# A recurrence and a feed-forward block in one kernel: keys kept in a ring in SBUF, block inverses taken round by round, weights with four landing buffers

## The chip, the cores and the metric

The kernel runs on one core of a Trainium2 chip. A core has TensorE (matrix products; its weight loads are a queue of their own in the profile), VectorE, ScalarE, GpSimd and SyncE (which issues the transfers here), each of which takes its instructions in order. The metric is the device time of one execution in microseconds (us), lower is better.

## The reference

Two blocks follow each other. The first is a recurrence over 768 positions with a 40x40 state for each of 4 x 8 heads; the second takes its output as 3072 rows of 320.

```python
for t in range(S):                                    # S = 768, heads of D = 40
    y[:, :, t] = einsum('bhd,bhde->bhe', rt, state)
    Sa = einsum('bhde,bhe->bhd', state, at)
    state = state * wt[:, :, None, :] - einsum('bhd,bhe->bhde', Sa, bt) \
            + einsum('bhd,bhe->bhde', vt, kt)
x = y.transpose(0, 2, 1, 3).reshape(B * S, H * D)     # (3072, 320)
h = x @ w_in                                          # d_ff = 1024
e = exp(h - max(h))
solu = h * (e / (sum(e) + 1e-9))
ln = (solu - mean(solu)) / sqrt(var(solu) + 1e-6) * g_ln
out = ln @ w_out
```

The arrays r, k, v, w, a, b come in 32-bit floats. w_in and w_out come as 64-bit floats, which the kernel reads as pairs of 32-bit words and converts itself.

## The kernel before

The 768 positions are cut into 12 rounds of 64 (chunks). The loop has 24 iterations: iteration i takes round i // 2 for two of the four batches. Within a chunk the recurrence becomes matrix products and the inverse of a unit triangular matrix of 64x64 for each head; its two 32x32 diagonal blocks are inverted on VectorE (`invert`), and the rest is put together by products (`solve`).

The parts of one iteration are Python generators; each `next` emits one piece, and a string of letters gives the order in which the pieces go into the engines' queues: r recurrence, f (and g) front, a attend (for i + 1), s solve (for i + 1), h hidden, I invert, W weights. `front` runs AHEAD = 7 iterations ahead and makes the keys `kx` (two scaled keys, A^T, decays); hidden and output run LAG = 4 iterations behind.

```python
AHEAD, LAG = 7, 4
kx_t = [const.tile([P, KW + G * AXW], FP32, name=f"kx{i}") for i in range(2)]

def spill(i):                     # keys go to DRAM ...
    d["kx_dram"] = dram.tile([P, KW + G * AXW], FP32, tag="kx_dram", name="kx_dram")
    nc.sync.dma_start(out=d["kx_dram"], in_=d["kx"])

def bring(i):                     # ... and come back when they are needed
    kx = two.tile([P, KW + G * AXW], FP32, tag="kxx", name="kxx")
    nc.sync.dma_start(out=kx, in_=d["kx_dram"])

def invert(number, got):          # rounds 0 and 1 alone on 64 partitions, then two rounds on 128
    # ... u = -nb, diagonal 1
    for j in range(1, Q - 1):     # Q = 32
        m = Q - 1 - j
        nc.vector.tensor_tensor(out=t, in0=nb[:, j:j + 1, j + 1:Q].to_broadcast([n_, j, m]),
                                in1=u[:, 0:j, j:j + 1].to_broadcast([n_, j, m]), op=ALU.mult)
        nc.vector.tensor_tensor(out=u[:, 0:j, j + 1:Q], in0=u[:, 0:j, j + 1:Q], in1=t, op=ALU.subtract)
        yield
    # ... transposed copy, both to DRAM, to be brought back in another layout

def weights():                    # 12 pieces of w_in, 16 of w_out
    def fetch(j):
        bits[j] = two.tile([P, 512], I64, tag=("e", "lnT")[j % 2], name="bits", bufs=1)
        # ... transfer of piece j into it
    fetch(0)
    fetch(1)
    yield
    for j, (dst, _, by) in enumerate(pieces):
        new = narrow(dst, bits[j], by)     # conversion: VectorE, ScalarE, then GpSimd
        # ... first half of new, second half of the piece before
        if j:
            fetch(j + 1)
        yield

def hidden(i):                    # two pieces h = x w_in (second with the maximum), then
    # yield; exponential (ScalarE); yield
    nc.vector.tensor_tensor(out=q, in0=h, in1=e, op=ALU.mult)
    for half in range(2):
        nc.vector.bn_stats(out=bs[:, half], in_=q[:, half * 512:half * 512 + 512])
    nc.vector.bn_aggr(out=mv, in_=bs)
    # ... four operations on one column; yield; ln; yield

STEADY = "r I f h r a f a h a r r h f r f h a s h a r s a"
EARLY = "r f r I W a f a g a I W r r g f r f I W a s g a r I W s g a"
# each iteration: turns(EARLY if i < LAG else STEADY, dict(I=count, W=3), **parts),
# then spill, readout(i), bring(i + 2), repack, scatter, rest of invert, output(i - LAG), store
```

In the profile the tensors carry these names: pcum, pcx, paT, pbT, pnt are products of front (its steps); px with sm and pu, psT, pnu, pst, plamu those of recurrence; pyo that of its crossed part and of readout; pkT, pvT, prT, ppsi, plamv, px with psi of attend; py, pz of solve; h, plnT, po of the feed-forward; bits are landed weights; blk, prod, u belong to invert.

Of the kernel before, what the change touches and what calls it, by code (L numbers as in the profile page):

```python
# [17 lines left out]
P = 128  # L18
Q = 32
L = 64  # L20
TILE_HEADS = ((0, 4, 3), (1, 5, 7), (2, 6))
AHEAD = 7
LAG = 4
# [30 lines left out]
def kernel(  # L54
# [22 lines left out]

# [12 lines left out]
    raw = ctx.enter_context(tc.tile_pool(name="raw", bufs=2))  # L90
    two = ctx.enter_context(tc.tile_pool(name="two", bufs=2))
    small = ctx.enter_context(tc.tile_pool(name="small", bufs=4))
    dram = ctx.enter_context(tc.tile_pool(name="dram", bufs=AHEAD + 2, space=bass.MemoryType.DRAM))
# [38 lines left out]
    kx_t = [const.tile([P, KW + G * AXW], FP32, name=f"kx{i}") for i in range(2)]  # L132
# [6 lines left out]
    tn_t = [const.tile([P, 2, G, Q], FP32, name=f"tinv{i}") for i in range(2)]  # L139
    sm_t = zeroed(nc.vector, "sm", [P, 2, G, 64], 2)  # L140
    st_t = [const.tile([P, 2, G, D], FP32, name=f"st{i}") for i in range(2)]
    nu_t = [const.tile([P, H, 64], FP32, name=f"nu{i}") for i in range(2)]
# [13 lines left out]
    def narrow(dst, land, by=None):  # L156
# [3 lines left out]
        flat = land.bitcast(I32)  # L160
        word = flat[0:n, 0:2 * width].rearrange("p (n two) -> p n two", two=2)
        low, hi = word[:, :, 0], word[:, :, 1]
        man, scale = flat[0:n, 1024 - width:1024], flat[0:n, 1024 - 2 * width:1024 - width]
# [15 lines left out]
    def weights():  # L179
# [18 lines left out]
        bits = {}  # L198

        def fetch(j):  # L200
            if j >= len(pieces):
                return
            dst, parts = pieces[j][:2]
            n, width = dst.shape
            to = dst
            if not exact:
                bits[j] = two.tile([P, 512], I64, tag=("e", "lnT")[j % 2], name="bits", bufs=1)
                to = bits[j][0:n, 0:width]
            row = 0
            for part in parts:  # L210
                nc.sync.dma_start(out=to[row:row + part.shape[0]], in_=part)
                row += part.shape[0]

        fetch(0)
        fetch(1)
        yield
        open_ = None
        for j, (dst, _, by) in enumerate(pieces):
            new = None
            if not exact:  # L220
                new = narrow(dst, bits[j], by)
            elif by is not None:
                nc.gpsimd.tensor_scalar(out=dst, in0=dst, scalar1=by[0], scalar2=None, op0=ALU.mult)
# [4 lines left out]
            if j:  # L228
                fetch(j + 1)
# [41 lines left out]
    def wide(name, bufs=2):  # L271
# [4 lines left out]
    blocks, inverse = {}, {}  # L276
# [25 lines left out]
    def group(n):  # L302

        return (n, 0, 1) if n < 2 else (1 + n // 2, n % 2, 2)

    def decay(i):

        d = st[i]
        lw, kx = lw_t[i % 2], kx_t[i % 2]
        d["kx"] = kx  # L310
        d["kb"], d["ax"] = kb, ax = split(kx)
        nc.scalar.activation(out=keyed(lw)[:, :, :, 0:D], in_=by_heads(given(i, "w")), func=AF.Ln)
# [21 lines left out]
    def homes(n, q, s=None):  # L334

        _, place, rounds = group(n)
        at = (q * rounds + place) * 2 * H + (s or 0) * H
        return slice(at, at + (H if s is not None else 2 * H))

    def front(i):  # L340
# [25 lines left out]
        if s == 0:  # L366
            of_round[n]["nt"] = two.tile([P, 2, 2, G, L], FP32, tag="nt", name="nt", bufs=4)
# [3 lines left out]
    def spill(i):  # L371

        d = st[i]
        d["kx_dram"] = dram.tile([P, KW + G * AXW], FP32, tag="kx_dram", name="kx_dram")
        nc.sync.dma_start(out=d["kx_dram"], in_=d["kx"])

    def scatter(n):

        number, place, _ = group(n)
        if place == 0:  # L380
            blocks[number] = dram.tile([P, Q, Q], FP32, tag="blk_dram", name="blk_dram", bufs=2)
        nt = of_round[n]["nt"].rearrange("q s p g t -> q (s p g) t")
        for q in range(4):
            nc.sync.dma_start(out=blocks[number][homes(n, q)].rearrange("h s t -> s h t"),
                              in_=nt[quarter(q), :, quarter(q % 2)])

    first = [two.tile([P, Q, Q], FP32, tag=tag, name=tag, bufs=1) for tag in ("blk", "u")]

    def gather(number):

        if number < 2:
            at = half(number)
            tiles = [x[at] for x in first]
        else:
            at = slice(0, P)
            tiles = [two.tile([P, Q, Q], FP32, tag=tag, name=tag, bufs=1) for tag in ("blk", "u")]
        nc.sync.dma_start(out=tiles[0], in_=blocks[number][0:at.stop - at.start])
        return tiles, at

    def invert(number, got):  # L400

        (nb, u), at = got
        n_ = at.stop - at.start
        flat = u.rearrange("p s t -> p (s t)")
        nc.vector.tensor_scalar(out=flat, in0=nb.rearrange("p s t -> p (s t)"), scalar1=-1.0, scalar2=None,
                                op0=ALU.mult)
        nc.vector.memset(flat[:, 0:Q * Q:Q + 1], 1.0)
        yield
        for j in range(1, Q - 1):
            m = Q - 1 - j  # L410
            t = two.tile([P, Q * Q // 4], FP32, tag="prod", name="prod", bufs=1)[at, 0:j * m] \
                .rearrange("p (c r) -> p c r", c=j)
            nc.vector.tensor_tensor(out=t, in0=nb[:, j:j + 1, j + 1:Q].to_broadcast([n_, j, m]),  # L413
                                    in1=u[:, 0:j, j:j + 1].to_broadcast([n_, j, m]), op=ALU.mult)
            nc.vector.tensor_tensor(out=u[:, 0:j, j + 1:Q], in0=u[:, 0:j, j + 1:Q], in1=t, op=ALU.subtract)  # L415
            yield
        nc.vector.tensor_copy(out=nb, in_=u.rearrange("p s t -> p t s"))
        inverse[number] = []
# [396 lines left out]
```

## Time and profile before

| | before |
|---|---|
| median of three runs | 1035.88 us (1030.49 to 1040.53) |
| span of the profiled run | 1030.6 us, mean granted TensorE clock 0.789 |
| TensorE, weight loads | 708.4 us busy (69%), 529.2 us (51%) |
| VectorE, ScalarE, GpSimd | 420.1 us (41%), 273.4 us (27%), 135.2 us (13%) |
| transfers | 106.75 MB, mean 104 GB/s |

The page cuts the span into 40 equal slices of 25.8 us; each digit is the busy share of a slice in tenths, for PEclk the clock that was granted to TensorE, in tenths of full speed.

```profile
PE   4248143541423869888788887888898888877875
DVE  2865112083221347433276332674337533332231
PEclk9657565755555889888988999788988888888988
DMA  9587613826142354463744636342534223020000
```

The rows are read against each other: a slice in which TensorE has a low digit and no other engine a high one is a slice in which all wait for something.

The costliest groups (line, engine, operation, out <- in with shapes, count | busy us, mean ns of one | idle us ahead of it, and what ended most of that):

```profile
L621 PE MATMUL h<-w_in,xT 120*128 120x512 f32 (+1 forms) x288 | 139.8, 624 | 9.8 <-DVE e L631 6.9
L661 PE MATMUL po<-w,lnT 128*128 128x320 f32 x384 | 112.0, 445 | 4.3 <-ACT lnT L657 4.0
L415 DVE TENSOR_TENSOR u<-u,prod 128x30 f32<-128x30 f32 (+29 forms) x210 | 74.3, 354 | 7.2
L413 DVE TENSOR_TENSOR prod<-blk,u 128x30 f32<-128x30 f32 (+29 forms) x210 | 72.5, 345 | 6.8
```

### The profile page before, as it was taken

The numbers are of one execution on the slowest core, as the hardware profiler recorded it, in microseconds if no ns is written. First come the engines' busy times: TensorE is split into PE (matmuls) and PEld (weight loads), VectorE is DVE, ScalarE is ACT, GpSimd is POOL, SyncE is SP. The second block draws the span as 40 slices with busy tenths as digits, with TensorE's granted clock in tenths as the row PEclk, the third lists the DMA queues.
The fourth block names the chain that finished last, engine by engine and source line by source line (L and its number), as shares of the span: only waits on it lengthen the run. The fifth ranks groups of instructions, "written<-read, shape, count | busy, mean of one in ns | idle before, by whom it ended". The sixth has DMA issues, their size and how long they took to land.

```text
span 1030.6 us, 27637 instructions
## 1 busy us (share of the span) xinstructions
PE 708.4 (69%) x12265; PEld 529.2 (51%) x12265; DVE 420.1 (41%) x941; ACT 273.4 (27%) x592; POOL 135.2 (13%) x202
## 2 busy tenths in 40 slices
PE   4248143541423869888788887888898888877875
PEld 3236133431322647676566665666566566655443
DVE  2865112083221347433276332674337533332231
ACT  3013133200432223223322333233332222221111
POOL 2102032101322110111011110111100000000000
PEclk9657565755555889888988999788988888888988
DMA  9587613826142354463744636342534223020000
GB/s 144 152 227 186 121 36 121 171 103 140 39 132 56 100 116 121 124 151 93 162 100 128 159 100 131 116 121 92 142 82 102 86 75 83 12 66 2 26 13 13
DMA packets 233862, 106.75 MB, mean 104 GB/s; under 512 B 216840, under 2 KB 223056, under 8 KB 227600
## 3 DMA queue, kind: packets, MB, share of 16 engines
q1 hardware_dynamic: 233600, 104.76, 40.9%
q8 instruction: 96, 1.57, 0.6%
q10 hardware_dynamic: 144, 0.23, 0.1%
q14 instruction: 22, 0.18, 0.1%
HBM read 62.30 MB, written 38.73 MB: 98 GB/s over the span
## 4 chain that ended last, share of the span: by engine, by line
PE 43%; DVE 14%; issue 13%; DMA 11%; SPq 9%; ACT 5%; POOL 4%; POOLq 0%; DVEq 0%; ACTq 0%
PE h L621 10%; PE po L661 7%; SPq L292 4%; PE px L467 4%; DMA bits<-in_moe_w_out_dram 4%; PE pyo L592 4%; DVE prod L413 2%; DVE u L415 2%; PE plamu L265 2%; PE pz L489 2%; PE plnT L656 2%; DMA bits<-in_moe_w_in_dram 2%; DMA blk<-blk_dram 2%; DVE e L647 2%; PE pst L565 2%
## 5 line engine op out<-in xcount | busy, mean ns | idle before, releaser
L621 PE MATMUL h<-w_in,xT 120*128 120x512 f32 (+1 forms) x288 | 139.8, 624 | 9.8 <-DVE e L631 6.9
L661 PE MATMUL po<-w,lnT 128*128 128x320 f32 x384 | 112.0, 445 | 4.3 <-ACT lnT L657 4.0
L661 PEld LDWEIGHTS po<-w,lnT 128*128 128x128 f32 x384 | 72.8, 194 | 38.5 <-ACT lnT L657 9.4
L621 PEld LDWEIGHTS h<-w_in,xT 120*128 120x128 f32 (+1 forms) x288 | 54.6, 199 | 64.5 <-issue 62.0
L624 DVE TENSOR_REDUCE nmax<-h 128x1 f32<-128x1024 f32 x24 | 29.3, 1222 | 117.7 <-PE h L621 117.5
L415 DVE TENSOR_TENSOR u<-u,prod 128x30 f32<-128x30 f32 (+29 forms) x210 | 74.3, 354 | 7.2
L413 DVE TENSOR_TENSOR prod<-blk,u 128x30 f32<-128x30 f32 (+29 forms) x210 | 72.5, 345 | 6.8
L326 PE MATMUL pcx<-cst,lw 128*128 128x132 f32 x192 | 38.4, 340 | 45.3 <-ACT kT L249 25.2
L514 PE MATMUL pyo<-rT,sT 64*64 64x64 f32 x704 | 30.3, 295 | 52.5 <-DVE psi L267 52.2
L326 PEld LDWEIGHTS pcx<-cst,lw 128*128 128x128 f32 x192 | 31.9, 235 | 50.9 <-ACT kT L249 28.5
L319 POOL TENSOR_TENSOR kx<-raw_b,inv 128x320 f32<-128x320 f32 x24 | 20.8, 865 | 260.1 <-ACT inv L317 248.5
L503 ACT ACTIVATE tinvT<-pz 32x256 f32<-32x256 f32 x48 | 17.9, 374 | 138.3 <-PE pz L489 138.0
L467 PE MATMUL px<-v,psi 64*64 64x40 f32 x768 | 46.4, 305 | 11.8 <-ACT tinvT L503 11.8
L572 POOL TENSOR_TENSOR st<-tot,kxx 128x320 f32<-128x320 f32 x20 | 14.9, 744 | 295.6 <-DVE tot L571 295.6
L599 DVE TENSOR_TENSOR x<-pyo,kxx 128x512 f32<-128x512 f32 x24 | 16.6, 691 | 89.6 <-PE pyo L592 89.6
L165 DVE TENSOR_SCALAR bits<-bits 128x160 int32<-128x160 int32 (+2 forms) x28 | 7.4, 264 | 111.7 <-DMA bits<-in_moe_w_out_dram 60.2
L514 PEld LDWEIGHTS pyo<-rT,sT 64*64 64x64 f32 x704 | 23.7, 192 | 55.8 <-DVE psi L267 55.3
L657 ACT COPY lnT<-plnT 128x512 f32<-128x512 f32 x48 | 26.4, 588 | 91.3 <-PE plnT L656 91.2
L467 PEld LDWEIGHTS px<-v,psi 64*64 64x64 f32 x768 | 42.8, 220 | 14.2 <-ACT tinvT L503 12.9
L265 PE MATMUL plamu<-rT,nuT 64*64 64x64 f32 x768 | 25.0, 298 | 29.8 <-DVE lamv L267 21.5
L532 DVE TENSOR_TENSOR x<-x_own,px 128x320 f32<-128x320 f32 x22 | 10.7, 485 | 73.7 <-PE px L530 73.7
L664 ACT COPY osb<-po 128x320 f32<-128x320 f32 x24 | 10.2, 425 | 108.0 <-PE po L661 57.6
(106 smaller groups left out, 1292.1 us busy)
## 6 DMA issues: line engine op xcount, KB each, us to landing
kx_dram<-kx SPq DMA_DIRECT2D x24, 1032.0 KB
kxx<-kx_dram SPq DMA_DIRECT2D x24, 1032.0 KB
raw_w<-in_w_dram SPq DMA_DIRECT2D x24, 160.0 KB
raw_b<-in_b_dram SPq DMA_DIRECT2D x24, 160.0 KB
raw_a<-in_a_dram SPq DMA_DIRECT2D x24, 160.0 KB
raw_k<-in_k_dram SPq DMA_DIRECT2D x24, 160.0 KB
v<-in_v_dram SPq DMA_DIRECT2D x24, 160.0 KB
r<-in_r_dram SPq DMA_DIRECT2D x24, 160.0 KB
```

What stands on the lines that cost most here:

```text
L265: nc.tensor.matmul(t[half(c), p, g * L:(g + 1) * L], lhsT=lhs[half(p), g, half(c)], rhs=rhs[half(p), g, half(c)], start=True, stop=True)
L292: nc.sync.dma_start(out=to[half(c)], in_=ap[2 * c:2 * c + 2, :, n * L:(n + 1) * L, :] .rearrange("b h t d -> t (b h) d"))
L326: nc.tensor.matmul(t[:, g * 132:g * 132 + 132], lhsT=pair(lw, 2 * j + g), rhs=cst[:, lo:lo + 132], start=True, stop=True)
L413: nc.vector.tensor_tensor(out=t, in0=nb[:, j:j + 1, j + 1:Q].to_broadcast([n_, j, m]), in1=u[:, 0:j, j:j + 1].to_broadcast([n_, j, m]), op ...
L415: nc.vector.tensor_tensor(out=u[:, 0:j, j + 1:Q], in0=u[:, 0:j, j + 1:Q], in1=t, op=ALU.subtract)
L467: nc.tensor.matmul(t[half(c), h * D:h * D + D], lhsT=psi[half(c), h // G, h % G, :], rhs=given(i, "v")[half(c), h, 0:D], start=True, stop= ...
L514: nc.tensor.matmul(d["y"][half(p), c, g * L:g * L + L], lhsT=d["sT"][half(z), c, m, half(p)], rhs=d["rT"][half(z), (G * p + g) // 2, half(c)],
L592: nc.tensor.matmul(t[half(p), c, g * L:g * L + L], lhsT=kb[half(c), j, 2 * g + p, :], rhs=lam[half(c), h % 2, h // 2, :], start=i < 2 and ...
L621: nc.tensor.matmul(h[:, hh], lhsT=of_round[i // 2]["xT"][0:n, kt, i % 2 * P:i % 2 * P + P], rhs=w_in[0:n, kt, hh], start=kt == 0, stop=kt ...
L624: nc.vector.tensor_reduce(out=nmax, in_=h, axis=AX.X, op=ALU.max, negate=True)
L657: nc.scalar.copy(out=lnT[:, fs.start:fs.stop].rearrange("p f t -> p (f t)"), in_=t)
L661: nc.tensor.matmul(o[:, 0:DM], lhsT=lnT[:, f, :], rhs=w2[:, f, :], start=f == 0, stop=f == NF - 1)
```

## The change

The change keeps the keys on the chip and orders the pieces anew.

- The keys kx live in a ring of AHEAD + 1 = 6 tiles (AHEAD is now 5), so that spill and bring go. To make room, several tiles have one buffer less (raw loads, psi, nuT, tot, sm, nu).
- The inverse is taken once per round (12 times). Each 32x32 block lies on two partitions, its even rows in the lower half of the partitions and its odd rows in the upper half, so one operation covers (j + 1) // 2 rows where it covered j.
- The weights have four landing quarters and two sets of temporaries, three loads are in flight ahead, and the pieces are spread over more iterations (LAG is now 6, so the feed-forward starts two iterations later).
- The feed-forward's product, statistics and small operations are pieces of their own; readout has a letter (y) within the order; the state's update comes after readout, and attend's psi and lamv come late.

```diff
-AHEAD = 7
-LAG = 4
+AHEAD = 5
+LAG = 6
-    raw = ctx.enter_context(tc.tile_pool(name="raw", bufs=2))
+    raw = ctx.enter_context(tc.tile_pool(name="raw", bufs=1))
-    kx_t = [const.tile([P, KW + G * AXW], FP32, name=f"kx{i}") for i in range(2)]
+    kx_t = [const.tile([P, KW + G * AXW], FP32, name=f"kx{i}") for i in range(AHEAD + 1)]
 ... weights
-                bits[j] = two.tile([P, 512], I64, tag=("e", "lnT")[j % 2], name="bits", bufs=1)
+            for tag in ("e", "lnT"):
+                x = two.tile([P, 512], I64, tag=tag, name="bits", bufs=1)
+                land += [x[:, 0:256], x[:, 256:512]]
+            temps = [two.tile([P, 2, 256], I32, tag=tag, name="parts", bufs=1) for tag in ("osb", "parts")]
-        fetch(0)
-        fetch(1)
+        for j in range(3):
+            fetch(j)
-                new = narrow(dst, bits[j], by)
+                new = narrow(dst, land[j % 4], temps[j % 2], by)
-            if j:
-                fetch(j + 1)
+            fetch(j + 3)
 ... spill and bring removed; gather brings a round's blocks twice, once for each half of the partitions
+        for p in range(2):
+            nc.sync.dma_start(out=nb[half(p)], in_=of_round[n]["blocks"])
 ... invert
-            m = Q - 1 - j
+            m, rows = Q - 1 - j, (j + 1) // 2
-                                    in1=u[:, 0:j, j:j + 1].to_broadcast([n_, j, m]), op=ALU.mult)
+                                    in1=u[:, 0:rows, j:j + 1].to_broadcast([P, rows, m]), op=ALU.mult)
+        nc.sync.dma_start(out=ut_dram, in_=ut)
+        for p in range(2):
+            nc.sync.dma_start(out=u_dram.rearrange("b (c z) t -> b c z t", z=2)[:, :, p], in_=u[half(p)])
 ... bring_inverse: tinv in four transfers where there were two, of 16 elements where there were 32
 ... recurrence: crossed part and lamu ahead of the state's update (they came after it)
 ... hidden
         nc.vector.tensor_tensor(out=q, in0=h, in1=e, op=ALU.mult)
+        yield
 ... bn_stats
+        yield
 ... order of the pieces
-    STEADY = "r I f h r a f a h a r r h f r f h a s h a r s a"
-    EARLY = "r f r I W a f a g a I W r r g f r f I W a s g a r I W s g a"
+    FIRST = "r f r I a f a g a r r g f r f I s g y s I r a g a I f g a"
+    EARLY = "r f I r a f a W a r r f r f I s W y s r W a a f a"
+    STEADY = "r I f h r a f a h a r r h f r f s h h y s h r a h a f a"
 ... loop
-            count = 5 if i < LAG else 5 if i % 4 == 1 else 10
+            if i % 2 and (i + 3) // 2 < NCH:
+                gather((i + 3) // 2)
+                inv = invert((i + 3) // 2)
+            turns(FIRST if i == 0 else EARLY if i < LAG else STEADY,
+                  dict(I=4 if i < LAG else 6 if i % 2 else 12), **parts)
+            steps(inv, 9 if i % 2 else 99)
+            if i < LAG:
+                steps(ws, 3)
```

## The prediction

> **What bounds the kernel now.** I first read the busy row of the page in slices. The first 13 of the 40 slices (0 to 325 us) have a near idle TensorE at about half clock; the rest is dense. So there are two problems. Then I cut the span at places found in the order of time: iteration 0 begins at 75 us, 1 at about 110, 2 at 179, 3 at 241, 4 at 325, and the tail after iteration 23 at 958. Columns: stretch, us, busy us of TensorE, its weight loads, VectorE, ScalarE, GpSimd, then granted clock, DMA share, GB/s.
>
> ```profile
> 121.00:179.00 58.00, 23.72 (x408) 20.21 (x412) 13.16 (x40) 20.22 (x54) 17.41 (x25) 0.59 0.20 70
> 179.00:241.00 62.00, 27.63 (x602) 22.86 (x601) 31.24 (x77) 9.84 (x21) 8.16 (x10) 0.67 0.54 137
> 241.00:325.00 84.00, 21.01 (x452) 18.37 (x452) 16.05 (x60) 26.21 (x66) 20.98 (x38) 0.54 0.39 96
> 325.00:958.00 633.00, 533.37 (x9790) 398.25 (x9791) 278.00 (x574) 181.00 (x375) 69.95 (x96) 0.86 0.40 102
> 958.00:1030.00 72.00, 51.64 (x146) 28.40 (x144) 20.37 (x36) 11.04 (x21) 2.19 (x4) 0.86 0.06 14
> ```
>
> No engine is busy in iterations 1 to 3: something is waited for. The waits of 110 to 325 us (line, waited for: total us, times, longest) and those of the DMA queue of 0 to 330 us name it:
>
> ```profile
> DVE bits L165 <- DMA bits<-in_moe_w_out_dram: 60.2, 15, 15.4
> DVE bits L165 <- DMA bits<-in_moe_w_in_dram: 51.5, 10, 18.7
> DVE u L405 <- DMA blk<-blk_dram: 25.9, 1, 25.9
> ```
> ```profile
> SPq L211 <- POOL w L176: 47.9, 13, 6.2
> SPq L211 <- POOL w_in L176: 43.6, 11, 6.1
> SPq L375 <- DVE kx L360: 34.5, 4, 15.0
> ```
>
> Two landing buffers make a ring: a load is issued when GpSimd has finished the last piece, and the conversion waits for the load. As all engines work in order, the whole iteration waits (112 us for 25 pieces).
>
> From 325 us TensorE is the bound, at 84% busy. The order of time of one fully clocked iteration shows its holes:
>
> ```profile
> 608.22 0.69 PE L265 MATMUL plamv<-rT,vT 64*64 64x64 f32 x32
> 610.84 0.46 PE L514 MATMUL pyo<-rT,sT 64*64 64x64 f32 x16 [1.93 <-DVE psi L267]
> 612.41 0.69 PE L265 MATMUL plamu<-rT,nuT 64*64 64x64 f32 x32 [1.11 <-DVE lamv L267]
> ```
>
> VectorE takes the product, both statistics and the small operations of the feed-forward in one block ahead of the masks of psi and lamv, and TensorE waits. In other iterations that hole also halves the clock (stretches of 2 us):
>
> ```profile
> 445.00:447.00 2.00, 0.97 (x38) 0.84 (x37) 1.84 (x7) 0.00 (x0) 0.98 (x3) 0.80 0.83 224
> 447.00:449.00 2.00, 1.13 (x44) 0.95 (x37) 1.11 (x2) 0.00 (x0) 1.11 (x1) 0.50 0.92 384
> 451.00:453.00 2.00, 2.00 (x64) 2.00 (x66) 0.00 (x0) 0.53 (x2) 0.00 (x0) 0.50 0.03 8
> ```
>
> [...] after 4 us at about half load the clock is 0.50 until about 456 us, and 32 products of 64x64 take 1.13 us there, not 0.69. [...] Here 30 elements take 0.15 us and 240 take 0.40: about 0.15 us are fixed, so halving the elements does not halve an inverse.
>
> **The change, part by part.**
>
> 1. Spill and bring removed: 24 + 24 transfers of 1032 KB, 49.5 of 106.75 MB. In steady state they lay beside other work. At the start they are on the path: the chain has 5.58 us for kx_dram at 22.9 and 6.81 us for kxx at 46.2.
>
> 2. Inverse by rounds. Before: 7 inverses, (74.3+72.5)/7 = 21.0 us each. The new form has 60 operations on about half the elements: 2 x 4960 elements at 1.04 ns fall to 5200, so 21.0 - 4.9 = 16.1 us. Twelve of them are 193 us for 147. Copies and fills add about 8. VectorE grows from 420 to about 475 us. On the path only the first counts: its 29 us (26 to 55) become about 20, though it must share the time with fronts 2 and 3, now not held by the spill. With bring and a second single inverse gone from the path, the first pu moves from 76 to about 61 us. (I place: nt of front 3 at 38, first inverse done at 49, its transfers 7 us, solve 4 us.)
>
> 3. Weights: 28 pieces, now three loads ahead and spread over iterations 0 to 5. GpSimd needs about 1.1 to 1.3 us per piece, so 7 us per iteration (six pieces) beside 5 of its own: no bound. The 112 us of waits go.
>
> 4. Early iterations. The anchor is iteration 0 before: two fronts and half an inverse took 75 to 100, 25 us, with TensorE mostly at half clock. I take 25 us for iteration 0 (61 to 86) and 29 for 1 to 5: TensorE's 15.4 us at full clock (26.3 of step 5 less h 5.3, plnT 1.1, po 4.5) become 25 at half clock (times 1.13/0.69), and the last inverse steps plus three pieces (7 us of VectorE) stand ahead of the next x0. 86 + 5 x 29 = 231 us at the start of iteration 6, where before the first with a feed-forward was at 325.
>
> 5. Steady order. Starts of successive groups in 594.7 to 625.4 us add up to 26.3 us of TensorE. I walked the new order through with these durations: exp ends, then the mask of lamu, product (1.2), statistics (1.3); meanwhile TensorE has bT, py, readout (2.0), pz, pst, psi to do. The psi mask is done at 19.5 us and its user starts at 20. The holes of 1.9 and 1.1 us go; short waits of 0.3 us (pcum, pcx, pnu, lnT) remain, about 1.3. So 28 us, for some 31 to 32 before and 37 where an inverse was gathered. The half-clock stretches should go with the holes. An inverse's 6 or 12 steps (3 to 7 us) fit ahead of the maximum at 10 us, where VectorE idled (7.83 us ahead of nmax in the iteration at 430).
>    Iterations 6 to 18: 13 x 28 = 364. 19 to 22 have no front (pcum 0.6, pcx 1.2, paT, bT, nt 0.6 each less): 4 x 24.5 = 98. The last, without attend and solve, is its feed-forward's own chain (about 15 us to the normalized tile) and output: 21.
>
> 6. LAG 6 moves two feed-forwards into the tail, where one takes about 16 us (h groups at 967.4, 982.7, 999.3), since the exponential stands in ScalarE's order behind the copy of the output before it: 72.6 + 32 = 105 us.
>
> Sum: 231 + 364 + 98 + 21 + 105 = 819. The timed median lay 5 us over the profiled span before: **823 us**.
>
> **Rivals.**
> (a) The start stays bound by handoffs. In odd iterations VectorE now waits early for the gather, which follows a scatter (3.5 us to issue, 2 to land) and its own 5 us, behind the inverse's stores and weight loads in one queue. I expect about 11 us, mostly hidden. If it holds 10 us more in each: 29 becomes 39, total 873. For it: the wait of 25.9 us above, from the same queue. Against: the long loads no longer precede the gather.
> (b) The holes only move: a two-bank PSUM buffer is now held through the whole readout, and pst waits for nu. If 2 us and the half clock stay, 31 us an iteration: 18 x 3, total 875.
> (c) VectorE becomes the bound: about 10 + 9 = 19 of 28 us in a steady iteration. Not by sum; only by a late gather in odd iterations (5 us x 6): 850.
> (d) The start's gain is repaid at the end: the tail is sure to cost 32 us, but not the 90 us that the start gains. Even with (a) and (b) in full the total is 823 + 50 + 54 = 927. For it: an earlier stage's gain is often taken back; against: the tail's length is known.
>
> **Range and chances.** The start has the largest error (195 to 265 us for the 231), the steady period the next (27.3 to 31, times 18). Delays that I have not seen are likelier than gains, so the range leans upward: 785 to 885. No rival, nor two of them, comes near 1015, so faster by over 2% has 0.97; 0.02 within; 0.01 slower.
>
> **What would show it.** The first h product at 231 us (step 4); no wait of VectorE for bits over a few us (3); the first pu near 61 (2); DMA bytes near 57 MB (1); VectorE about 475 us (2); periods between h groups of 28 us, no psi wait ahead of pyo, clock above 0.95 from there to the tail (5); a tail of six at about 16 us (6). I would be wrong if VectorE waits for blk in each odd iteration, if the clock stays at 0.86, or if the first h comes after 265 us.

## The result, and the profile after

| | before | after | the prediction |
|---|---|---|---|
| median | 1038.13 us (1030.49 to 1040.53) | 862.57 us (851.79 to 864.45) | 823, range 785 to 885 |
| ratio after to before, 95% interval | | 0.8298 [0.8214, 0.8382] | |
| span of the profiled run | 1030.6 us | 859.1 us | 819 |
| mean granted clock | 0.789 | 0.884 | over 0.95 in the steady part |
| VectorE busy | 420.1 us | 474.0 us | about 475 |
| transfers | 106.75 MB | 59.20 MB | near 57 MB |

(The median of before here includes the run beside the changed kernel.) The direction and most of the sum hold; 40 us of the gain did not come. The page of the changed kernel, in 40 slices of 21.5 us:

```profile
PE   5428366465578998898899899888988899788684
DVE  2564375575567475674674764756756633322421
PEclk9668577587599999999999979989998999889988
DMA  6576436436434355253253361462232211010000
```

TensorE is now dense from the 13th slice (258 us) on, and there the clock is at 9 in 21 of the 28 slices. Ahead of that it is mostly at 3 to 7 beside a clock of 5 to 8: less empty than it was, but still waiting. In the tail it dips to 6 and 4.

The start of the product pu marks each iteration. Busy time between such marks, columns as in the windows of before (us; TensorE, weight loads, VectorE, ScalarE, GpSimd; granted clock, DMA share, GB/s): iteration 1, the thirteen iterations 6 to 18, and the tail.

```profile
104.00:138.40 34.40, 19.69 (x451) 16.67 (x450) 20.51 (x65) 13.60 (x33) 11.29 (x16) 0.65 0.41 93
...
258.00:638.40 380.40, 340.32 (x6784) 249.04 (x6784) 242.70 (x640) 129.33 (x271) 55.41 (x75) 0.96 0.41 74
...
752.00:859.00 107.00, 78.94 (x240) 44.56 (x240) 30.56 (x54) 17.42 (x33) 3.28 (x6) 0.88 0.06 15
```

A steady iteration lasts 380.4/13 = 29.3 us, of which TensorE works 340.3/13 = 26.2. The whole steady excess is idle time of TensorE: 3.1 us an iteration, not 1.3. In iteration 1, no engine is busy for more than 60% of the time: something is waited for, as in the kernel before, but for less long. The first product h, forecast for 231 us, comes at 252.4 (327.3 before).

What TensorE and VectorE wait for in the first 280 us (engine, line, waited for: total us, times, longest):

```profile
PE px L506 <- POOL sm L501: 40.3, 4, 12.1
...
PE pg L181 <- DMA g_rows<-in_moe_g_ln_dram: 9.1, 1, 9.1
...
DVE parts L163 <- DMA bits<-in_moe_w_in_dram: 7.5, 2, 6.0
```

The 112 us of VectorE's waits for landed weights are 7.5. In their place TensorE waits for sm, the state scaled by GpSimd, four times 8 to 12 us. GpSimd's own order of time ahead of the longest of these:

```profile
129.70 0.72 POOL L174 TENSOR_TENSOR w_in<-parts 120x256 f32<-120x256 f32 x1 [7.36 <-DVE parts L171]
...
134.18 0.73 POOL L174 TENSOR_TENSOR w_in<-parts 120x256 f32<-120x256 f32 x1 [0.83 <-DVE parts L171]
134.85 0.45 POOL L343 COPY a<-raw_a 128x320 f32<-128x320 f32 x1
135.26 0.74 POOL L501 TENSOR_TENSOR sm<-st,kx 128x320 f32<-128x320 f32 x1
```

sm itself takes 0.74 us, and the state st that it scales is ready at 120.02 us, but it is queued behind three weight pieces and not taken up while GpSimd stands idle. The first of these waits 7.36 us for VectorE, which has the remaining steps of the inverse ahead of its part of the piece:

```profile
123.23 0.24 DVE L397 TENSOR_TENSOR prod<-blk,u 128x92 f32<-128x92 f32 x1
...
128.53 0.28 DVE L399 TENSOR_TENSOR u<-u,prod 128x120 f32<-128x120 f32 x1
...
129.13 0.42 DVE L171 SCALAR_TENSOR_TENSOR parts<-bits,parts 120x256 int32<-120x256 int32 x1
```

A wait for a transfer has become a wait for a place in a queue.

In iterations 6 to 18 the waits of pyo for psi and of plamu for lamv are gone. More than half of TensorE's idle time there (22.9 of 40.1 us) has no releaser:

```profile
327.42 0.51 PE L464 MATMUL pz<-tinvT,y_mid 32*32 32x32 f32 x21 [1.29 <-issue]
...
331.15 0.51 PE L263 MATMUL plamv<-rT,vT 64*64 64x64 f32 x19 [1.02 <-issue]
```

"Issue" is time in which the engine waited for nothing that the profile shows. Of stalls of 0.6 us and more, those under "issue" add up to 38 us in the whole run, against 5.7 us before; these are the sums in the texts below. In each, one of 3.0 us is another thing: it precedes an h of the tail (at 811.98 us), exactly where the h products around it wait 3.0 us for VectorE's e. Without it there are 29 such stalls with 35 us, for 2 with 2.7 us before, and so they are counted from here on. In the trace of the changed kernel they lie 256 recorded TensorE instructions apart, or a multiple of that, and the page lists a queue of the kind "instruction" with 96 packets and 1.57 MB; the last section has what was measured of both.

### The profile page after: what moved, and what is told of

The parts are those of the page before. It is cut to its first block, busy times and chain, and to the rows that moved or that the text cites. A ratio compares the mean times of both kernels' runs of the same rounds, so it can differ in the third digit from the quotient of the medians.

```text
span 859.1 us, 28102 instructions
## 1 busy us (share of the span) xinstructions
PE 663.2 (77%) x12265; PEld 481.8 (56%) x12265; DVE 474.0 (55%) x1279; ACT 273.6 (32%) x592; POOL 135.4 (16%) x206
## 2 busy tenths in 40 slices
DMA packets 265978, 59.20 MB, mean 69 GB/s; under 512 B 254328, under 2 KB 260544, under 8 KB 265856
## 3 DMA queue, kind: packets, MB, share of 16 engines
q8 instruction: 96, 1.57, 0.8%
## 4 chain that ended last, share of the span: by engine, by line
PE 63%; DVE 12%; issue 9%; ACT 8%; DMA 4%; SPq 3%; POOL 1%; POOLq 0%; ACTq 0%; DVEq 0%
PE h L597 14%; PE po L639 12%; PE pst L548 3%; PE pyo L568 3%; PE plnT L634 3%; PE pcum L312 3%; PE pcx L322 2%; PE px L442 2%; PE pu L514 2%; DVE prod L397 2%; DVE u L399 2%; PE pz L464 2%; PE pnt L263 2%; PE pbT L245 2%; PE pnu L532 2%
## 5 line engine op out<-in xcount | busy, mean ns | idle before, releaser
L399 DVE TENSOR_TENSOR u<-u,prod 128x30 f32<-128x30 f32 (+4 forms) x360 | 97.6, 271 | 12.4
L397 DVE TENSOR_TENSOR prod<-blk,u 128x30 f32<-128x30 f32 (+4 forms) x360 | 98.2, 273 | 10.9
L622 POOL TENSOR_TENSOR rs<-c,mhalf 128x1 f32<-128x1 f32 x24 | 13.2, 548 | 386.8 <-DVE c L621 386.8
L506 PE MATMUL px<-sm,kx 64*64 64x40 f32 x704 | 16.7, 243 | 40.3 <-POOL sm L501 40.3
L355 DVE TENSOR_TENSOR kx<-paT,kx 128x512 f32<-128x512 f32 x24 | 16.5, 691 | 51.1 <-PE paT L354 41.1
L634 PE MATMUL plnT<-cst,e 128*128 128x128 f32 x192 | 34.2, 327 | 12.4 <-DVE e L625 11.4
L607 DVE TENSOR_TENSOR e<-h,e 128x1024 f32<-128x1024 f32 x24 | 29.3, 1220 | 25.4 <-ACT e L604 25.4
L506 PEld LDWEIGHTS px<-sm,kx 64*64 64x64 f32 x704 | 14.0, 149 | 48.3 <-POOL sm L501 40.9
L312 PE MATMUL pcum<-lw,cst 128*128 128x320 f32 x48 | 24.4, 597 | 19.2 <-ACT lw L308 19.2
L442 PE MATMUL px<-v,psi 64*64 64x40 f32 x768 | 36.2, 259 | 3.5 <-issue 3.1
L634 PEld LDWEIGHTS plnT<-cst,e 128*128 128x128 f32 x192 | 26.3, 168 | 20.7 <-issue 12.9
```

The source lines that it names most:

```text
L312: nc.tensor.matmul(t[:, 0:DM], lhsT=c_("cum_in"), rhs=lw[:, :, 0:D], start=True, stop=True)
L399: nc.vector.tensor_tensor(out=u[:, 0:rows, j + 1:Q], in0=u[:, 0:rows, j + 1:Q], in1=t, op=ALU.subtract)
L442: nc.tensor.matmul(t[half(c), h * D:h * D + D], lhsT=psi[half(c), h // G, h % G, :], rhs=given(i, "v")[half(c), h, 0:D], start=True, stop= ...
L506: nc.tensor.matmul(t[half(c), p, g * D:g * D + D], lhsT=d["aT"][half(p), g, half(c)], rhs=sm[half(p), c, g, 0:D], start=True, stop=True)
L634: nc.tensor.transpose(out=t[:, j * P:(j + 1) * P], in_=ln[:, f * P:(f + 1) * P], identity=ident)
```

## The experiments

My first theory was that the gain is the sum of the prediction's parts, and that the missing 40 us are (1) weight pieces in the way of the early iterations and (2) these stalls without a releaser, which grow when TensorE gets its operands in time. The rivals: the order of the pieces brings little, the depth of the landing ring all of the start; VectorE's longer inverse holds everything; removed traffic brings nothing.

The four runs of the changed kernel lie 12.7 us apart, so small differences of medians say little. Stretches in which several kernels have the same order give a finer measure: iteration 6 starts at 254.5 to 258.0 us (changed kernel, e1, e3, e5, e8), iterations 6 to 18 take 377 to 387 us (changed kernel, e2, e5, e7), the last iteration and the tail 119 to 124 us (changed kernel, e2, e3, e4, e6, e7).

Runs, medians and ratios to the kernel before measured beside them:

| run | median, us | ratio [95%] |
|---|---|---|
| e1 steady order of before | 907.17 | 0.8775 [0.8752, 0.8798] |
| e2 two landing buffers | 871.87 | 0.8436 [0.8390, 0.8481] |
| e3 traffic put back | 883.96 | 0.8552 [0.8528, 0.8575] |
| e4 half of the inverse's steps | 839.45 | 0.8124 [0.8095, 0.8153] |
| e5 tail order | 833.90 | 0.8066 [0.8024, 0.8109] |
| e6 sm placed early | 850.31 | 0.8219 [0.8178, 0.8260] |
| e7 weights fetched early | 853.45 | 0.8246 [0.8193, 0.8299] |
| e8 po between short products | 836.95 | 0.8093 [0.8058, 0.8129] |
| b1 kernel before, four landing buffers | 983.39 | 0.9539 [0.9479, 0.9599] |
| c1 start and tail | 814.76 | 0.7888 [0.7841, 0.7935] |
| c2 c1 and po between | 819.36 | 0.7928 [0.7894, 0.7962] |
| c3 c2, early placement at the start only | 827.78 | 0.8013 [0.7960, 0.8066] |

**e1: the order of before in the steady iterations**, all else as changed.

```diff
-    STEADY = "r I f h r a f a h a r r h f r f s h h y s h r a h a f a"
+    STEADY = "r I f h r a f a h a r r h f r f h h h a s h a r s a y f"
 ... and, from iteration LAG on, the crossed part and lamu after the state's update
```

> The changed kernel with one part undone: from iteration 6 on, the pieces stand as before (the feed-forward's product, statistics and small operations in one block ahead of psi and lamv, state's update ahead of lamu, readout last). Theory A (step 5 of the prediction: the new order closes two holes of TensorE and with them the half clock): the waits of pyo on psi and of plamu on lamv come back, the period goes from 29.2 to about 31.5 us and the clock of the steady part from 0.97 to about 0.9; 18 iterations make +40 us, 900 us in all. Theory B (the holes only moved: TensorE's idle time named 'issue', 38 us in the changed kernel and 6 us before, took their place): the issue time falls below 15 us, the period stays below 30, total within 15 us of the changed kernel's 863.

Measured: 44.6 us more than the changed kernel. Iterations 6 to 18 take 413.6/13 = 31.8 us, so 33 of the 45 us lie in them. TensorE's waits in 258 to 660 us name the old holes:

```profile
PE pyo L490 <- DVE psi L265: 22.5, 13, 1.9
PE plamu L263 <- DVE lamv L265: 13.7, 13, 1.2
```

That is 36.2/13 = 2.8 us an iteration, the 1.9 + 1.1 of the prediction. How it becomes 33 us is seen beside the window from 258.00 us of the changed kernel:

```profile
255.80:669.40 413.60, 363.13 (x6788) 273.03 (x6788) 244.45 (x640) 129.01 (x271) 56.80 (x75) 0.89 0.38 68
```

TensorE's idle time is 50.5 us for 40.1, only 10 us more, because the new order has 22.9 us of stalls under "issue" where the old one has 1.0. The other 23 us are busy time, 363.1 us for 340.3: the same products at a clock of 0.89 for 0.96. Theory A holds, the clock included, and B in part: step 5's mechanism is right, and some of what it won is paid again under another name.

**e2: two landing buffers, with the fetches placed as in the kernel before** (one load ahead once the first two are used up), and the pieces spread as changed.

```diff
-            to = dst if exact else land[j % 4][0:dst.shape[0], 0:dst.shape[1]]
+            to = dst if exact else land[j % 2][0:dst.shape[0], 0:dst.shape[1]]
-        for j in range(3):
+        for j in range(2):
-            fetch(j + 3)
+            if j:
+                fetch(j + 1)
```

> The changed kernel with two landing buffers for the weights and one load ahead, all else as changed. Theory A (step 3: prefetch took away the waits for landed weights): VectorE waits for bits again, some 2 us for each of 28 pieces, early iterations grow from 31-34 to about 40 us, +45 us, 908 us. Theory B (in the early iterations GpSimd's order sets the pace, px waits 40 us in all for sm behind the conversions, loads are hidden anyway): at most +10 us.

Measured: 9.3 us more, and the intervals of the two ratios nearly touch. In the trace, iteration 6 begins at 270.2 us, 12 us later than as changed and clear of the 254.5 to 258.0 us above. VectorE waits for bits again, 36.9 us from 60 to 270 us:

```profile
DVE parts L163 <- DMA bits<-in_moe_w_out_dram: 20.5, 8, 4.2
DVE parts L163 <- DMA bits<-in_moe_w_in_dram: 16.4, 7, 5.7
```

TensorE's own waits for sm grow by 15.6 of these 36.9 us, from 40.3 to 55.9. Theory B is nearer: once the pieces are spread, the deeper ring is worth some 12 us.

**b1: the deeper ring, with its second set of temporaries, alone**, in the kernel before, whose pieces stay crowded into iterations 1 and 3.

```diff
-                bits[j] = two.tile([P, 512], I64, tag=("e", "lnT")[j % 2], name="bits", bufs=1)
+ ... four quarters in the two tiles of before, piece j in land[j % 4]; two sets of temporaries
-        fetch(0)
-        fetch(1)
+        for j in range(3):
+            fetch(j)
-            if j:
-                fetch(j + 1)
+            fetch(j + 3)
```

> The kernel before with one part of the change alone: four landing quarters, two sets of temporaries and three loads ahead; the places of the pieces, spill and bring, the inverse and the order stay. Theory A, that the depth of the ring was the cause of the 112 us of waits for bits: those waits fall to under 40 us, iterations 1 and 3 shrink by 25 to 35 us each, total 970 to 990. Theory B, that the cause was that the pieces follow each other closely in two iterations, where any ring runs dry and the conversion itself (VectorE, ScalarE and GpSimd in turn, over 3 us a piece) sets the pace: the waits take other names (GpSimd's parts), total 1015 to 1035.

Measured: 983.39 us, 51 us below the kernel before. That is theory A's range. VectorE's waits for bits from 60 to 330 us fall from 111.7 us in 25 times to 36.0 in 4. With e2 this shows that the parts do not add: the deeper ring is worth 51 us where the pieces are crowded and about 12 where they are spread. Either remedy takes most of the same wait: 36.0 us of it are left with the ring, 36.9 with the spreading (e2), 7.5 with both. (e2 kept the second set of temporaries, so what share of the 51 us is theirs is not shown.)

**e3: the traffic put back**, without anyone waiting for it. From iteration 6 on each new kx is copied to DRAM and the one before copied from DRAM to DRAM.

```diff
+    def spill(i):
+        away[i] = dram.tile([P, KW + G * AXW], FP32, tag="kx_dram", name="kx_dram", bufs=4)
+        nc.sync.dma_start(out=away[i], in_=kx_t[i % (AHEAD + 1)])
+    def bring(i):
+        back = dram.tile([P, KW + G * AXW], FP32, tag="kx_back", name="kx_back", bufs=2)
+        nc.sync.dma_start(out=back, in_=away[i])
```

> The changed kernel with the traffic of the keys put back from iteration 6 on: each front's keys are written to DRAM (1032 KB) and those of the iteration before are copied from there to another place in DRAM; nothing waits for the copies. 13 + 13 transfers, about 27 MB more moved. Theory A (step 1: in steady state spill and bring lay beside other work): no change, within 1% of 863 us. Theory B (transfers delay what TensorE waits for, among it the fetch of its own instructions): TensorE's issue time rises from 38 to 55 us or more and the time by 15 us or more.

Measured: 21.4 us more, with 85.62 MB moved for 59.20. No instruction waits for a copied key. TensorE's waits from 255 to 630 us are these:

```profile
PE plamv L263 <- issue: 10.0, 4, 4.6
PE pst L558 <- issue: 6.8, 5, 2.7
```

Issue stalls of 0.6 us and more rise from 35 to 53 us over the run, single ones to 4.6 us, and the steady period to 406.1/13 = 31.2 us. In it TensorE is idle for 55.5 us instead of 40.1 and busy for 350.6 instead of 340.3, at a clock of 0.93 for 0.96. Theory B's figures hold: issue time of 55 us or more (53 and the 3 of the tail), 15 us or more in all. That it is the fetch of instructions which the transfers delay is not shown. Step 1 had put this traffic "beside other work"; it costs TensorE time without appearing as a transfer that anyone waits for.

**e4: the odd steps of every inverse left out** (it computes another inverse; only the time is of interest).

```diff
+            if j % 2:
+                yield
+                continue
```

> Leaves out every second round of each inverse (the rounds with odd j), so half of its VectorE operations: VectorE's busy time falls from 474 to about 378 us. The output is not the reference's. Theory A (the prediction: only the first inverse and some of the early iterations have it on their path): 8 us at the first inverse, 1 to 2 us in each early iteration, 0 in the steady ones: -15 us, 848. Theory B (rival c: VectorE bounds): the steady period falls from 29.2 to 28 or less by it, -35 us or more.

Measured: 23.1 us less. VectorE's busy time falls by 94 us (474.0 to 379.8), the first pu comes at 62.2 for 65.9, iteration 6 at 240.2 for 258.0. Iterations 6 to 18 stay as they were: 383.8/13 = 29.5 us for 29.3. The 17.8 us gained up to there are all that the two profiled runs differ by (841.4 for 859.1). So theory A: VectorE does not set the steady period (rival (c) falls); the inverse matters only at the start, where the weight pieces queue behind it.

**e5: the tail's output behind the next h pair and its exponential.** `o` is the product po with its copy by ScalarE.

```diff
-            turns("h o h o h h h h h", {}, h=hidden(m), o=before)
+            turns("h o h h o h h h h", {}, h=hidden(m), o=before)
```

> The changed kernel, in the tail (the last six feed-forwards) the exponential stands ahead of the output of the tile before in ScalarE's order, not behind the copy of that output. Theory A (step 6: the tail's period of 15 us is set by that order): the period falls to about 12 us, -15 us, 848. Theory B (h's single PSUM tile and the half clock set it): less than -5 us.

The tail of the changed kernel in TensorE's order of time shows what this is aimed at:

```profile
783.30 2.81 PE L597 MATMUL h<-w_in,xT 120*128 120x512 f32 x6 [3.02 <-DVE e L607]
...
797.60 2.81 PE L597 MATMUL h<-w_in,xT 120*128 120x512 f32 x6 [2.97 <-DVE e L607]
```

Each h waits 3 us for VectorE's product, which waits for an exponential that stands behind the copy of an output. Measured: 28.7 us less; a feed-forward of the tail takes 11.0 us where it took 14.3 to 16.2, and all of those waits but the first are gone. The last iteration and the tail take 100.9 us for 118.6, so 18 us come from the new order, close to theory A's 15. The other 10 lie ahead of the tail, where both kernels have the same order; it does not account for them. The mechanism of step 6 is right, and it could have been ordered away.

**e6: the next iteration's sm ahead of the three weight pieces** at the end of iterations 0 to 5; the remaining inverse steps stay ahead of it.

```diff
                 steps(inv, 9 if i % 2 else 99)
                 if i < LAG:
+                    begin(i + 1)
+                    started = recurrence(i + 1)
+                    steps(started, 1)        # sm, now a piece of its own
                     steps(ws, 3)
```

> The changed kernel with the next iteration's sm (GpSimd) and front's first piece put ahead of the three weight pieces at the end of iterations 0 to 5. Theory A (GpSimd's order is what makes the early iterations 31 to 34 us where 29 were predicted): the wait of px for sm falls from 40 us to under 10 and most of it is won, -25 us, 838. Theory B (VectorE is as late: its last inverse steps and the pieces stand ahead of x0 as well): the wait moves to pu for x0, at most -8 us.

Measured: 12 us less by the medians, with overlapping intervals; iteration 6 starts at 250.1 us, 8 us earlier than as changed. The wait for sm is gone from TensorE's list in the first 280 us; the next thing that VectorE's queue holds back heads it, as theory B had it:

```profile
PE pu L516 <- DVE x L510: 32.2, 5, 9.8
```

**e7: the first weight loads and the load of g_ln issued ahead of iteration 0, the product pg placed within it.**

```diff
-        pg = bank("pg")
-        nc.tensor.transpose(out=pg[:, 0:NF], in_=g_rows, identity=ident[0:NF, 0:NF])
 ... moved behind the first yield of weights()
+            if i == 0:
+                steps(ws, 1)
```

> The changed kernel with the first three weight pieces and the gains asked for at the start of iteration 0, not at its end, where the page shows waits for g_rows (9 us) and for lw behind the pieces (5.6 us). Theory A (these waits are on the path): iteration 0 falls from 38 to 25 us as predicted, -12 us, 850. Theory B (the conversions themselves and the inverse hold it): -4 us or less.

Measured: 9 us less by the medians, again with overlapping intervals. The trace is clearer: iteration 0 takes 33.3 us for 38.1, iteration 6 starts at 248.3, and the wait of 9.1 us for g_rows is gone, though the wait for lw behind it grows from 5.6 to 11.0 us.

**e8: the feed-forward's output products between readout and pz**, so that TensorE's stretch of short products (32 to 64 columns) is broken by sixteen long ones.

```diff
-    STEADY = "r I f h r a f a h a r r h f r f s h h y s h r a h a f a"
+    STEADY = "r I f h r a f a h a r r h f r f s h h y o s h r a h a f a"
```

> The changed kernel with the output's product po (16 wide products, 4.6 us, few instructions) taken into the next iteration, between readout and pz, amid some 900 short instructions of TensorE. Theory A (TensorE waits for its own instructions, 256 at a time, where it runs through the short ones faster than they come: the issue stalls lie exactly 256 instructions or multiples apart): the issue time falls from 38 to under 15 us, -15 us, 848. Theory B (the stalls follow the transfers alone, or VectorE's inverse steps, no longer covered by po, hold x0): no gain, or up to +10.

Measured: 25.6 us less. Theory A: issue stalls fall from 35 to 9.8 us over the run and the steady period to 361.5/13 = 27.8 us. Of the 19 us gained there, TensorE's idle time gives 7 (33.3 us for 40.1) and its busy time 12 (328.2 for 340.3, at a clock of 0.98 for 0.96). Part of the gain is lost to waits for VectorE, of which this one, from 258 to 619 us, is the largest:

```profile
PE pu L514 <- DVE x L508: 11.2, 7, 2.8
```

**c1, c2, c3: put together.** c1 joins e5 and e7 and places the next iteration's whole first piece (sm, px, x0) and its front's first piece (a logarithm and a copy) ahead of the inverse's rest and the weight pieces. c2 adds e8. c3 is c2 with that early placement only while weights are loaded, and with the next front's first exponential placed early too.

```diff
 ... c1
+            begin(i + 1)
+            if more:
+                started = recurrence(i + 1)
+                steps(started, 2)         # sm; px and x0
             steps(inv, 9 if i % 2 else 99)
             if i < LAG:
                 steps(ws, 3)
-            begin(i + 1)
 ... c3: the added lines only for i < LAG, with one more step of the front;
 ... from i = LAG on at the end of the iteration, as before
```

> Three edits together that touch the two ends only: the tail's output behind the next h pair and its exponential (alone 29 us less than the changed kernel's 863), the first weight loads issued ahead (alone 9 us less), and the next iteration's first piece (masked scores, px, x0) and its front's loads placed ahead of the iteration's remaining inverse steps and weight pieces. In the run that moved only the masked scores, the wait for them went and one of pu for x0 on VectorE (32 us) came in its place. Theory A, that VectorE's order behind the weight pieces is what held the early iterations after the scores were there: x0 is now ahead as well, both waits go, the early periods fall from 31 to 34 us to 25 to 29, first h near 220 to 230, total 795 to 805. Theory B, that the early iterations are bound by all they have to do (weights, inverse and front on VectorE and GpSimd at a half clock of TensorE), and only the name of the wait changes again: another wait takes the 30 us (fronts, kT or blk), the edit brings only the 38 of the other two and 5 to 10 more, 815 to 825.

> The kernel before this in the list, with po's products placed between readout and pz as well, so that TensorE's stretch of short products is broken by long ones (alone: 26 us less than the changed kernel's 863, and the time that TensorE waited for no one 38 to 12.7 us). Theory A, that this gain lies in the steady iterations and adds to that of the two ends: 20 to 27 us below the kernel before this in the list, 770 to 785, with issue time under 18 us. Theory B, that with the ends tightened VectorE's operations (x and kx, which took 23 us of waits when po was moved alone) hold TensorE in its place: at most 8 us below.

> The kernel with tail order, early fetch and po between (819 us), but the next iteration's first piece goes ahead of the inverse's remaining steps only while weights are loaded (iterations 0 to 5), with the next front's decay products and exponentials ahead of the weight pieces as well, since TensorE now waited 8 to 10 us there for the exponential inv behind ScalarE's part of the weights; from iteration 6 on the order is that of the run with po between. Theory A, that the early placement cost the steady iterations what it had given the early ones (VectorE's kx then stands behind more work: 30.6 us of waits for kx where the run with po alone had 10.9): steady periods 27.6 to 28.2 for 28.9, waits for inv go (38 us, of which half may turn into other waits), first h 215 to 235, total 775 to 795. Theory B, that the early iterations stay at 31 to 34 us as in every run so far because VectorE, ScalarE and GpSimd hand each weight piece on in turn, and only the steady part gains: 800 to 810.

(The "masked scores" of these texts are sm, the scaled state.)

Measured: c1 814.76 us, the best version here, 48 us below the changed kernel, just under the 815 to 825 of theory B. Iteration 0 falls to 22.0 us, but iterations 1 to 4 stay at 31 to 34, and iterations 1 to 5 take 161.1 us, 7 more than as changed. sm and x0 no longer hold TensorE; "pcx waits for ScalarE's inv" does, 38 us in five times. c2 is no faster than c1 (theory B; the intervals overlap): iterations 6 to 18 take 28.9 us for c1's 28.4. There the time under "issue" falls from 20.2 to 2.8 us, and 25.9 us of waits of py for VectorE's kx (c1: 2.7) more than make up for it. c3 is what neither theory expected: it gets the steady period back (28.1 us, as theory A said) and loses the start: iterations 1 to 4 take 38.0, 38.9, 35.4 and 34.3 us. The wait has moved once more, to ScalarE's copy kT (40.9 us in 16 times), which now stands behind the weights:

```profile
99.08 1.25 PE L322 MATMUL pcx<-cst,lw 128*128 128x132 f32 x4 [8.56 <-ACT kT L247]
```

So in four placements (after, e6, c1, c3) the early iterations waited for GpSimd's sm, VectorE's x0, ScalarE's inv and ScalarE's kT in turn, each queued behind the same weight pieces. Moving one operation ahead changes the name of the wait more than its length. What the best place for the pieces is stays open; in each of the four, iterations 1 to 4 kept a mean of 30.9 us or more.

## Why the prediction was right, and where it was off

The iterations' marks give the account of the 40 us that the span lay above the sum of 819:

| stretch | predicted | measured | difference |
|---|---|---|---|
| up to the first pu | 61 | 65.9 | +4.9 |
| iteration 0 | 25 | 38.1 | +13.1 |
| iterations 1 to 5 | 145 | 154.0 | +9.0 |
| iterations 6 to 18 | 364 | 380.4 | +16.4 |
| iterations 19 to 22 | 98 | 102.1 | +4.1 |
| the last iteration and the tail | 126 | 118.6 | -7.4 |

**Step 1, spill and bring: half right.** The start's waits for kx_dram and kxx are gone. The bytes fall to 59.2 MB for 57: 48 tiles of 1032 KB (of 1024 bytes each) are 50.7 MB, not 49.5, and the blocks gathered twice bring 3.1 MB more. "In steady state they lay beside other work" is what failed: e3 puts about half of the bytes back (26.4 of 50.7 MB), off every chain of waits, and the kernel is 21 us slower. So, in the new order at least, the removed traffic has a share in the steady period, and the sum gave it none. That is no part of the 40 us, since it made the change better than its reason said.

**Step 2, the inverse: right.** The groups of the changed kernel:

```profile
L399 DVE TENSOR_TENSOR u<-u,prod 128x30 f32<-128x30 f32 (+4 forms) x360 | 97.6, 271 | 12.4
L397 DVE TENSOR_TENSOR prod<-blk,u 128x30 f32<-128x30 f32 (+4 forms) x360 | 98.2, 273 | 10.9
```

(97.6 + 98.2)/12 = 16.3 us an inverse for the predicted 16.1: subtracting the elements at their measured rate (0.21 us for 58 and 0.40 for 240 before, 1.04 ns an element) and keeping the fixed part was sound. The new form shows that part again: 15 elements take 0.18 us, 128 take 0.29. (The prediction's 0.15 us for 30 elements is that of single operations; their mean is 0.18 to 0.20, and with it the fixed 0.15 comes out.) The first pu came 4.9 us late; e4 returns 3.7 of them with half of the steps.

**Step 3, weights: the result right, the cause shared.** The 112 us of waits went (7.5 remain). I named two causes, and e2 and b1 weigh them: with the pieces spread the ring's depth is worth about 12 us, without spreading 51. "GpSimd needs about 1.1 to 1.3 us per piece ... no bound" counted its work (1.06 us for a piece of w_out and 1.47 for one of w_in by the groups of before, 11.3 us busy of 34.4 in iteration 1) and not its order: sm stands behind the pieces, and GpSimd itself waits for VectorE.

**Step 4, early iterations: the step that failed most, 22 us.** The 29 us rested on TensorE at half clock for 25 us plus a few for x0. Measured in iterations 1 to 5: TensorE is busy 94.9/5 = 19.0 us, at clocks of 0.65 to 0.94, so it was less slow than I took it to be, and its idle time is 59/5 = 12 us, not 4. The two errors, 6 us down and 8 up, nearly cancel: that the mean of 30.8 us came so near to 29 is luck. I had placed the three pieces at the end of an iteration ahead of x0 as 7 us of VectorE's work; it is a chain of VectorE, ScalarE, VectorE and GpSimd behind up to 5.6 us of inverse steps (from 123.2 to 128.8 us in the stretch shown), which the next sm then joins. Iteration 0 missed most (38.1 us for 25), since its anchor in the kernel before had no weight pieces in it: TensorE waits there 9.1 us for g_rows and 5.6 for lw behind it, 14.7 us in all, more than the whole excess. (By the marks of pu, iteration 1 of that kernel starts at 100.7 us, not at about 110; the anchor of 25 us is right.) With the loads ahead and x0 moved (c1) it took 22.0 us.

**Step 5, steady order: mechanism right, the remainder mis-sized.** TensorE's 26.3 us per iteration were measured as 26.2, the holes at psi and lamv went, and the clock is 0.96. e1 confirms the mechanism with 33 us in these iterations, 10 of idle time and 23 of the slower clock. That the holes are what halves the clock was my reading of the stretch from 445 us of before (0.80, then 0.50); e1 shows the waits (36.2 us) and the lower clock (0.89 for 0.96) coming back together, not what lowers it. TensorE's idle time, "short waits of 0.3 us ... about 1.3", was 3.1: 22.9/13 = 1.8 us of it are stalls under "issue", a term that the sum did not have, and the rest is the 1.3 predicted. e8 takes most of these stalls away (-19 us in the same iterations).

**Step 6, the tail: right in kind, size a little high.** A feed-forward takes 14.3 to 16.2 us for "about 16"; with the last iteration 118.6 us for 126 (up to 123.7 in runs with the same order).

**The rivals.** (a) happened in part, though not through the gather: VectorE's waits for blk are short (5.9 us in two times from 104 to 258 us). (b) did not happen: pst waits for no nu. (c) did not happen (e4). (d) falls too: iteration 6 starts at 258.0 us, where iteration 4 of before started at 331.4, and the tail gave back the 35 us by which it grew (107 for 72), not the gain. Of the signs of being wrong none came: the first h is ahead of 265 us, and the steady clock is 0.96, not 0.86. The range held because it leaned upward for delays not seen, which is what came: the queue behind the weight pieces and the stalls under "issue".

## What to carry to other kernels

When a wait for a transfer is taken away, look at what is queued behind the work that it feeds: where an engine takes its work in the order of its queue, as GpSimd did here, a short operation that others need (0.74 us here) can stand 8 to 12 us behind work that nobody needs yet, and moving it alone only promotes its neighbour. Two remedies for one wait (a deeper ring, pieces spread out) must not be added up; price each with the other in place. And when TensorE has all its operands, mix long products into stretches of short ones and place a store or copy behind the next exponential: 26 us over the run and 18 in the tail here for a changed letter or two, though the first of these gave nothing more once the two ends had been moved as well.

## What the runs showed of the hardware

In the trace of the changed kernel, TensorE's stalls without a releaser stand at fixed counts of its instructions, and each ends soon after a packet of an instruction queue has landed. I read them as waits for its own instructions; no view of the profile names what they wait for. The page lists 96 packets in that queue, 1.57 MB in all, so 16.4 KB each. The 2 x 12265 products and weight loads that it lists are 255.5 a packet, 258 with the 217 instructions of TensorE's sequencer that the trace records too. Counted with those, the two stalls shown, before 327.42 and 331.15 us, lie 256 recorded instructions apart, and all 29 counted above lie a multiple of 256 apart, to within two. A block is here a stretch of 256 instructions, counted from one of these places. The trace also has the times of the packets (us):

| | the block before starts | the packet starts | it has landed | the stall ends | its length |
|---|---|---|---|---|---|
| as changed | 323.22 | 325.12 | 326.15 | 327.42 | 1.29 |
| as changed | 327.42 | 328.57 | 329.68 | 331.15 | 1.02 |

In all 29 stalls the last packet to land starts 0.6 to 2.4 us after the first instruction of the block before, takes 0.9 to 1.5 us, and the stall ends 1.24 to 1.64 us after it has landed. TensorE worked the block before these stalls off in 2.4 to 3.8 us, in the stretches of short products; at 44 of the other 66 places where a block begins, the packet had landed more than 5 us before. In e3 the stalls of 1.71 and 4.60 us, before 580.57 and 588.16 us, lie 128 products apart, which is 256 instructions with their weight loads: the longest stall stands at such a place too. With long products between (e8), 9 stalls with 9.8 us are left. What decides when a packet starts, and why the stalls are longer beside other traffic, is not shown.
